# One decode layer on one core: 64 value rows multiplied on GpSimd, 8 key rows there, the head maximum by a VectorE transpose, one weight load cut by partitions

## The chip, the cores and the metric

The kernel runs on one core of a Trainium2 chip. The metric is the device time of one execution in microseconds; the kernel before has a median of 1319.2 us over 3 runs (1319.14 to 1319.23). Everything else comes from one execution that the hardware profiler recorded.

## The reference, cut to what matters

A decode step of one transformer layer with adaptive layer norm, batch 4, one token each, everything in float32:

```python
mod = (silu(c) @ w_mod).reshape(4, 6, 1, 512)            # sa, ca, ga, sb, cb, gb
h = layernorm(x) * (1 + ca) + sa
q = (h @ wq) -> (4, 32 heads, 1, 128)
scores = einsum("bhqd,bhkd->bhqk", q, k_cache) * 128 ** -0.5   # k_cache (4, 32, 4096, 128)
o = einsum("bhqk,bhkd->bhqd", softmax(scores), v_cache)        # v_cache (4, 32, 4096, 128)
x = x + ga * (o.reshape(4, 1, 4096) @ wo)
h = layernorm(x) * (1 + cb) + sb
x = x + gb * (silu(h @ w1) @ w2)                               # w1 (512, 1792), w2 (1792, 512)
```

The two caches hold 537 of the 567 MB that are read. Each cache element is used once: a key row of 128 floats gives one score, a value row is scaled by one weight and added up.

## The kernel before, in words

The caches are cut into 32 tiles each. Tile n stands for four heads (HP) of one batch row; t, b = n // 4, n % 4. A tile is 128 partitions x 128 rows x 128 floats, 64 KB in each partition and 8.4 MB in all. A partition holds 128 positions ("rows", index j) of one head; 32 partitions in a row belong to the same head. Three such buffers (the pool `kv`, class `Slot`) take turns, in the order k0, k1, v0, k2, v1, k3, ... So a key tile goes into the buffer of a value tile two steps older, and a value tile into that of the key tile just worked off. All loads are issued by SyncE (SP), in order, one whole tile at a time (`load_k`, `load_v`, `fetch`); an issue waits until the buffer is free.

The program's loop over n, whose order is the order on every engine, does in step n:

- Keys. Each row is multiplied by the query (`mult`) and summed over its 128 floats (`red`). GpSimd multiplies the first NA = 32 rows with a copy of the query in SBUF (`qw`), VectorE the other 96 with the query in PSUM (`qb`), and VectorE does all the sums into `sc[n]`. Steps 0 and 1 use NL = 56 rows in place of NA.
- Values of step n - 1. With `first(n)` = 14 groups of JJ = 4 rows, the first NV = 56 rows are scaled by their weights in place: rows 0 to 47 on GpSimd (one multiply), rows 48 to 55 on ScalarE (`vmult`). GpSimd then adds rows onto rows (28, 12, 8, 4 rows) until four are left, and TensorE sums these over the partitions in one matmul with `hs` (`vsum`). The other 72 rows go straight through TensorE: one matmul for each group of four (`pv`), with the weights spread into `pz` by GpSimd (in `softexp`). In the last two tiles, `first` is 0 and TensorE does all 128 rows.
- Softmax. `rowmax` gives a maximum for each partition; `bmax` transposes it on TensorE into PSUM, `negmax` takes the maximum of each head's 32 partitions and picks and negates it with the mask `hn` (three VectorE instructions); ScalarE does the exponentials (`softexp`).
- At three steps of four VectorE also drains or spreads a finished group of outputs (`gather`, `norm`, `spread`).

After the last key tile, SP loads `wo` in three pieces and the feed-forward weights `w12` in nine (w1 in the first two, then w2 in pieces of whole 512-column chunks, 256 KB each). TensorE matmuls named `busy` only fill time. The loop's last steps and the end of the program (projection, layer norm, the two feed-forward matmuls) run while these loads land; the last matmuls, of the second feed-forward matrix, take one chunk after the other.

Of the kernel before, what the change touches and what calls it, by code (L numbers as in the profile page):

```python
# [9 lines left out]
F32 = mybir.dt.float32  # L10
AF = mybir.ActivationFunctionType
ALU = mybir.AluOpType
AX = mybir.AxisListType
# [4 lines left out]
def kernel(  # L18
# [10 lines left out]
    nc = tc.nc  # L29
    P = 128  # L30
    B, H, S, Dh = kc.shape
    D = wo.shape[1] * P // (H * Dh)
    F = w12.shape[1] * P // (2 * D)
    G = 4
    W = P // G
    HP = 4
    QW = P // HP
# [6 lines left out]
    JJ = 4  # L44
# [4 lines left out]
    NK = D // P  # L49
    NI = F // P  # L50
    FG = F // G
    NA = 32
    NL = 56
    NV = 56
    NP = 48
    SCALE = 1.0 / math.sqrt(Dh)
    EPS = 1e-5
    N = B * NT
    SLOT = NJ * Dh

    const = ctx.enter_context(tc.tile_pool(name="const", bufs=1))
    kv = ctx.enter_context(tc.tile_pool(name="kv", bufs=3))
    work = ctx.enter_context(tc.tile_pool(name="work", bufs=2))
# [3 lines left out]
    def psum(shape, tag, bufs):  # L67
        return ps.tile(shape, F32, tag=tag, name=tag, bufs=bufs)
# [15 lines left out]
    def fetch(t, src, *cuts):  # L84
        for lo, hi in zip(cuts, cuts[1:]):
            nc.sync.dma_start(t[:, lo:hi], src[:, lo:hi])  # L86

    kt, vt = {}, {}

# [6 lines left out]
    def load_k(n, *cuts):  # L96
        load(kt, kc, "k", n, *cuts)

    def load_v(n):
        load(vt, vc, "v", n)  # L100
# [22 lines left out]
    ident = const.tile([P, P], F32, name="ident")  # L123
# [9 lines left out]
    avg = const.tile([P, G, W], F32, name="avg")  # L133
    for g in range(G):
        nc.vector.tensor_scalar(avg[:, g, :], sel, 1.0 / G, None, op0=ALU.mult)
    hm = const.tile([P, HP], F32, name="hm")
    nc.vector.tensor_reduce(hm, i4, axis=AX.X, op=ALU.add)
    hn = const.tile([P, HP], F32, name="hn")
    nc.vector.tensor_scalar(hn, hm, -1.0, None, op0=ALU.mult)
    jm = const.tile([P, JJ], F32, name="jm")  # L140
    nc.vector.tensor_reduce(jm, ident.rearrange("p (k j) -> p j k", j=JJ), axis=AX.X, op=ALU.add)
    xm = const.tile([P, B], F32, name="xm")
# [15 lines left out]
    hs = const.tile([P, W + E], F32, name="hs")  # L158
# [87 lines left out]
    for k in range(NK):  # L246
        for ch in range(H * Dh // CW):
            i, g = divmod(ch, G)
# [7 lines left out]
    for i in range(2):  # L256
        for u in range(HP):
            o = ZB - QW * u - G * B * i
# [9 lines left out]
    def make_qb(n):  # L268
        if n % B == 0:
            m = work.tile([P, B, Dh], F32, tag="o", name=f"qm{n}", bufs=1)  # L270
            for b in range(B):
                nc.scalar.activation(m[:, b, :], qn, AF.Copy, scale=sel[:, n + b : n + b + 1])  # L272
            p = psum([P, B, Dh], "q", 2)
            nc.tensor.matmul(p, blk.rearrange("p i x -> p (i x)"), m, start=True, stop=True)  # L274
            for b in range(B):
                qb[n + b] = p[:, b, :]
        qw[n] = work.tile([P, Dh], F32, tag="qw", name=f"qw{n}")
        nc.scalar.activation(qw[n], qb[n], AF.Copy)  # L278

    sc, nm, po, rs = {}, {}, {}, {}  # L280

    def mult(eng, src, n, lo, hi):
        eng.tensor_mul(  # L283
            kt[n][:, lo:hi, :], kt[n][:, lo:hi, :], src[n].unsqueeze(1).to_broadcast([P, hi - lo, Dh])
        )

    def red(n, lo, hi):
        nc.vector.tensor_reduce(sc[n][:, lo:hi], kt[n][:, lo:hi, :], axis=AX.X, op=ALU.add)  # L288

    def rowmax(n):  # L290
        nm[n] = work.tile([P, 1], F32, tag="rm", name=f"rm{n}")
        nc.vector.tensor_reduce(nm[n], sc[n], axis=AX.X, op=ALU.max)  # L292

    def bmax(n):
        p = psum([P, P + HP], "mx", 2)
        nc.tensor.transpose(p[:, :P], nm[n].to_broadcast([P, P]), ident)  # L296
        nm[n] = p

    def negmax(n):
        m = nm[n][:, P:]  # L300
        nc.vector.tensor_reduce(m, nm[n][:, :P].rearrange("p (i x) -> p i x", i=HP), axis=AX.X, op=ALU.max)  # L301
        nc.vector.tensor_mul(m, m, hn)
        nm[n] = work.tile([P, 1], F32, tag="nm", name=f"nm{n}")
        nc.vector.tensor_reduce(nm[n], m, axis=AX.X, op=ALU.add)  # L304

    def softexp(n):
        t, b = divmod(n, B)
        if b == 0:
            rs[t] = work.tile([P, B], F32, tag="rs", name=f"rs{t}")
        nc.scalar.activation(sc[n], sc[n], AF.Exp, bias=nm[n], accum_out=rs[t][:, b : b + 1])  # L310
        for h in range(2):
            f = min(max(first(n) - HG * h, 0), HG)
            m = HG - f
            if not m:
                continue
            nc.gpsimd.tensor_mul(  # L316
                pz[h][:, f * W : HG * W].rearrange("p (g x) -> p g x", g=m)[:, :, E:].rearrange("p g (i j) -> p g i j", i=HP),
                sc[n][:, JJ * (HG * h + f) : HG * JJ * (h + 1)].rearrange("p (g j) -> p g j", j=JJ)
                .unsqueeze(2).to_broadcast([P, m, HP, JJ]),
                hm.unsqueeze(1).unsqueeze(3).to_broadcast([P, m, HP, JJ]),  # L320
            )

    def first(n):
        return NV // JJ if n < N - 2 else 0

    def vmult(n):
        if first(n):
            v = vt[n]
            for j in range(NP, NV):
                nc.scalar.activation(v[:, j, :], v[:, j, :], AF.Copy, scale=sc[n][:, j : j + 1])  # L330
            nc.gpsimd.tensor_mul(  # L331
                v[:, :NP, :], v[:, :NP, :], sc[n][:, :NP].unsqueeze(2).to_broadcast([P, NP, Dh])
            )
            for m, lo in ((28, 28), (12, 16), (8, 8), (JJ, JJ)):
                nc.gpsimd.tensor_add(v[:, :m, :], v[:, :m, :], v[:, lo : lo + m, :])  # L335

    def vsum(n):
        t, b = divmod(n, B)
        q, a = divmod(b, 2)
        o = (1 - a) * E  # L340
        nc.tensor.matmul(  # L341
            po[t, q][0:W, :], hs[:, o : o + W], vt[n][:, :JJ, :].rearrange("p j d -> p (j d)"),
            start=False, stop=a == 1,
        )

    def pv(n):
        t, b = divmod(n, B)
        q, a = divmod(b, 2)
        if a == 0:
            po[t, q] = psum([P, JJ * Dh], "po", 2)  # L350
        f = first(n)
        for j in range(f, NG):
            g = j % G
            h, u = divmod(j, HG)
            o = u * W + (1 - a) * E
            nc.tensor.matmul(  # L356
                po[t, q][W * g : W * (g + 1), :],
                pz[h][:, o : o + W],
                vt[n][:, JJ * j : JJ * (j + 1), :].rearrange("p j d -> p (j d)"),
                start=(a == 0 and j < f + G), stop=(a == 1 and j >= NG - G and (g > 0 or not f)),  # L360
            )
# [25 lines left out]
    def sums(t):  # L387
        p = psum([P, B], "mx", 2)
        if t < TA:
            nc.tensor.matmul(p[W * t : W * (t + 1)], b8.rearrange("p i x -> p (i x)"), rs[t], start=True, stop=True)  # L390
        else:
            nc.tensor.matmul(p, blk.rearrange("p i x -> p (i x)"), rs[t], start=True, stop=True)
        rd[t] = p
# [53 lines left out]
    for n in range(N):  # L447
        t, b = divmod(n, B)
        if n + 1 < N:
            load_k(n + 1)  # L450
        else:
            load_v(n)
        if t and b == 1:
            sums(t - 1)
        sc[n] = work.tile([P, NJ], F32, tag="sc", name=f"sc{n}")
        w, m = (NJ // 2, NL // 2) if n == 0 else (NJ, NL) if n == 1 else (NJ, NA)
        for lo in range(0, NJ, w):
            mult(nc.gpsimd, qw, n, lo, lo + m)
            mult(nc.vector, qb, n, lo + m, lo + w)
            if n + 1 < N and not lo:  # L460
                make_qb(n + 1)
            if n:
                vmult(n - 1)
                pv(n - 1)
            red(n, lo + m, lo + w)
        for lo in range(0, NJ, w):
            red(n, lo, lo + m)
        if n + 1 < N:
            load_v(n)
        else:  # L470
            so = Slot("wo")
            wat, wot = so.take(RA, D), so.take(NT - TA, R, D)
            fetch(so.t, wo, 0, RA * D, SLOT - R * D, SLOT)
            s2 = Slot("w12")
            w1t = s2.take(NK, F)
            w2t = s2.take(NI, D)
            fetch(s2.t, w12, 0, 3 * F, *(NK * F + i * D for i in (0, 5, 8, 10, 11, 12, 13, 14)))
        rowmax(n)
        bmax(n)
        if n and first(n - 1):  # L480
            vsum(n - 1)
        negmax(n)
        softexp(n)
        if b == 3:
            gather(t, 0)
        if n == N - 1:
            sums(t)
            norm(t)
        if t and b == 1:
            gather(t - 1, 1)  # L490
            norm(t - 1)
        if t and b == 2:
            spread(t - 1)
# [25 lines left out]
    for g in range(G):  # L519
        o = g % 2 * P  # L520
# [71 lines left out]
```

## Time and profile before

| what | value |
|---|---|
| median of the runs shown | 1319.2 us |
| the profiled execution's own time | 1318.86 us |
| its span, first to last instruction | 1317.0 us |
| busy share of the span | DVE (VectorE) 79%, POOL (GpSimd) 82%, PE (TensorE) 27%, ACT (ScalarE) 10% |
| DMA queue of the loads | 99.6% of 16 DMA engines' span, 431 GB/s over the span |

The span is what the trace covers; 1.86 us of the execution lie outside it. "Idle before" in a group of instructions is the time in which the engine had nothing to run ahead of them, with what ended it. The time to landing of a load counts from its issue, so it holds the time that the load queued behind others.

### The profile page before, as it was taken

How to read it: one execution, taken by the hardware profiler on the slowest of the kernel's cores; microseconds unless marked ns; L12 is line 12 of the kernel's file. 1: busy time of each engine (PE TensorE's matmuls, PEld its weight loads, DVE VectorE, ACT ScalarE, POOL GpSimd, SP SyncE). 2: the span in 40 equal slices, each digit the busy share in tenths (PEclk: the TensorE clock that was granted, in tenths of full speed). 3: DMA queues.
4: the chain of work that ended last, by engine and by line, in shares of the span. 5: the costliest groups of instructions: out<-in, count | busy, mean ns of one | idle time of the engine just before them, and what ended most of it. 6: DMA issues, size and time to landing. Idle time of an engine off the chain costs nothing.

```text
span 1317.0 us, 5073 instructions
## 1 busy us (share of the span) xinstructions
PE 359.7 (27%) x1756; PEld 95.2 (7%) x1756; DVE 1045.5 (79%) x357; ACT 125.8 (10%) x408; POOL 1080.1 (82%) x257
## 2 busy tenths in 40 slices
PE   3301322221222232122322122132312213221258
PEld 1100000000000000000000000000000000000013
DVE  2597788988878998788898888789887878978762
ACT  1100110010001101011100100000100010000001
POOL 0459888888988888998888899888889888888910
PEclk9856666656666665666665566666556666655669
DMA  9999999999999999999999999999999999999998
GB/s 415 440 420 444 428 435 434 426 442 434 430 440 428 438 435 428 438 434 432 430 442 432 430 439 432 434 434 430 438 432 432 438 432 434 436 432 438 428 426 349
DMA packets 11433, 567.63 MB, mean 431 GB/s; under 512 B 1280, under 2 KB 1296, under 8 KB 2192
## 3 DMA queue, kind: packets, MB, share of 16 engines
q1 hardware_dynamic: 11408, 567.31, 99.6%
q8 instruction: 14, 0.23, 0.1%
q14 instruction: 11, 0.09, 0.0%
HBM read 567.30 MB, written 0.01 MB: 431 GB/s over the span
## 4 chain that ended last, share of the span: by engine, by line
DMA 50%; DVE 27%; POOL 19%; PE 2%; issue 1%; ACT 0%; SPq 0%; DVEq 0%; POOLq 0%
DMA k<-in_A_k_cache_dram 23%; DMA v<-in_A_v_cache_dram 21%; DVE sc L288 16%; DVE k L283 11%; POOL v L335 11%; POOL v L331 8%; DMA w<-in_B_w_dram 3%; DMA wq<-in_A_wq_dram 3%; PE po L341 1%; PE q L249 1%; PE mx L259 0%; ACT qm L272 0%; PE q L274 0%; SPq L86 0%; PE od L378 0%
## 5 line engine op out<-in xcount | busy, mean ns | idle before, releaser
L288 DVE TENSOR_REDUCE sc<-k 128x96 f32<-128x12288 f32 (+3 forms) x66 | 553.1, 8422 | 4.1
L283 DVE TENSOR_TENSOR k<-k,q 128x12288 f32<-128x12288 f32 (+2 forms) x33 | 408.3, 12372 | 183.1 <-DMA k<-in_A_k_cache_dram 168.1
L335 POOL TENSOR_TENSOR v<-v 128x3584 f32<-128x3584 f32 (+1 forms) x120 | 443.8, 3698 | 9.4
L331 POOL TENSOR_TENSOR v<-v,sc 128x6144 f32<-128x6144 f32 x30 | 313.8, 10460 | 103.4 <-DMA v<-in_A_v_cache_dram 103.4
L283 POOL TENSOR_TENSOR k<-k,qw 128x4096 f32<-128x4096 f32 (+2 forms) x33 | 296.4, 8982 | 31.4 <-ACT qw L278 31.4
L356 PE MATMUL po<-v,pz 128*32 128x512 f32 x1208 | 216.3, 839 | 335.6 <-DMA v<-in_A_v_cache_dram 335.6
L341 PE MATMUL po<-v,hs 128*32 128x512 f32 x60 | 57.4, 1061 | 413.8 <-POOL v L335 413.8
L330 ACT ACTIVATE v<-v,sc 128x128 f32<-128x128 f32 x240 | 73.6, 389 | 199.3 <-DMA v<-in_A_v_cache_dram 199.3
L356 PEld LDWEIGHTS po<-v,pz 128*32 128x32 f32 x1208 | 56.1, 148 | 500.8 <-issue 482.3
L296 PE MATMUL mx<-ident,rm 128*128 128x128 f32 x32 | 12.7, 396 | 175.7 <-DVE rm L292 175.7
L278 ACT ACTIVATE qw<-q 128x128 f32<-128x128 f32 x32 | 8.9, 278 | 525.6 <-DVE k L283 424.0
L316 POOL TENSOR_TENSOR pz<-sc,hm 128x32 f32<-128x32 f32 (+1 forms) x64 | 26.7, 438 | 30.4 <-ACT sc L310 30.4
L310 ACT ACTIVATE sc<-sc,nm 128x128 f32<-128x128 f32 x32 | 12.9, 402 | 367.9 <-DVE nm L304 367.9
L341 PEld LDWEIGHTS po<-v,hs 128*32 128x32 f32 x60 | 5.4, 140 | 421.5 <-POOL v L335 421.5
L301 DVE TENSOR_REDUCE mx<-mx 128x4 f32<-128x128 f32 x32 | 9.6, 300 | 17.8 <-PE mx L296 17.8
L367 DVE TENSOR_TENSOR o<-po,jm 128x512 f32<-128x512 f32 x16 | 10.9, 681 | 13.6 <-PE po L356 13.6
L296 PEld LDWEIGHTS mx<-ident,rm 128*128 128x128 f32 x32 | 5.2, 163 | 203.9 <-issue 162.1
L373 DVE TENSOR_REDUCE s<-o 128x128 f32<-128x512 f32 x16 | 16.5, 1034 | 0.6
L274 PE MATMUL q<-qm,blk 128*128 128x512 f32 x16 | 15.6, 1073 | 1.7 <-ACT qm L272 1.7
L200 PE MATMUL q<-wm 128*32 128x512 f32 x48 | 8.9, 668 | 18.9 <-DVE wm L184 18.9
L190 POOL COPY wm<-wm 128x16 f32<-128x16 f32 x1 | 0.2, 212 | 16.0 <-DMA wm<-in_head_dram 16.0
L499 PE MATMUL q<-mod,ident 128*128 128x512 f32 (+2 forms) x24 | 10.7, 554 | 0.0
(114 smaller groups left out, 164.9 us busy)
## 6 DMA issues: line engine op xcount, KB each, us to landing
k<-in_A_k_cache_dram SPq DMA_DIRECT2D x2, 4096.0 KB, 51.1
wm<-in_head_dram SPq DMA_DIRECT2D x1, 6160.0 KB, 17.7
wo<-in_A_wo_dram SPq DMA_DIRECT2D x1, 4096.0 KB, 18.1
wo<-in_A_wo_dram SPq DMA_DIRECT2D x1, 3072.0 KB, 25.0
w<-in_B_w_dram SPq DMA_DIRECT2D x1, 2688.0 KB, 33.1
w<-in_B_w_dram SPq DMA_DIRECT2D x1, 1280.0 KB, 37.3
wo<-in_A_wo_dram SPq DMA_DIRECT2D x1, 1024.0 KB, 27.0
w<-in_B_w_dram SPq DMA_DIRECT2D x4, 256.0 KB, 17.6
```

The costliest lines, as they stand in the source:

```text
L249: nc.tensor.matmul(pq[i][W * g : W * (g + 1), :], hT[:, k, :], wqt[:, k, ch * CW : (ch + 1) * CW], start=k == 0, stop=k == NK - 1,)
L274: nc.tensor.matmul(p, blk.rearrange("p i x -> p (i x)"), m, start=True, stop=True)
L283: eng.tensor_mul(kt[n][:, lo:hi, :], kt[n][:, lo:hi, :], src[n].unsqueeze(1).to_broadcast([P, hi - lo, Dh]))
L288: nc.vector.tensor_reduce(sc[n][:, lo:hi], kt[n][:, lo:hi, :], axis=AX.X, op=ALU.add)
L296: nc.tensor.transpose(p[:, :P], nm[n].to_broadcast([P, P]), ident)
L316: nc.gpsimd.tensor_mul(pz[h][:, f * W : HG * W].rearrange("p (g x) -> p g x", g=m)[:, :, E:].rearrange("p g (i j) -> p g i j", i=HP), sc[n ...
L330: nc.scalar.activation(v[:, j, :], v[:, j, :], AF.Copy, scale=sc[n][:, j : j + 1])
L331: nc.gpsimd.tensor_mul(v[:, :NP, :], v[:, :NP, :], sc[n][:, :NP].unsqueeze(2).to_broadcast([P, NP, Dh]))
L335: nc.gpsimd.tensor_add(v[:, :m, :], v[:, :m, :], v[:, lo : lo + m, :])
L341: nc.tensor.matmul(po[t, q][0:W, :], hs[:, o : o + W], vt[n][:, :JJ, :].rearrange("p j d -> p (j d)"), start=False, stop=a == 1,)
L356: nc.tensor.matmul(po[t, q][W * g : W * (g + 1), :], pz[h][:, o : o + W], vt[n][:, JJ * j : JJ * (j + 1), :].rearrange("p j d -> p (j d)") ...
L373: nc.vector.tensor_reduce(s, o.rearrange("p j d -> p d j"), axis=AX.X, op=ALU.add)
```

## The change

Four edits. `hm` is also given 64 bytes in place of 16, and `hn` is gone; the tile buffers start at the same addresses as before.

- Keys: NA = 8, so VectorE multiplies 120 rows of a tile and GpSimd 8 (steps 0 and 1 stay at 56).
- Values: GpSimd multiplies NV = 64 rows in tiles 0 to 29 and adds 32, 16, 8 and 4 rows; the last add writes to a tile of its own, `vs`, which `vsum` reads. ScalarE scales none. TensorE does 64 rows through `pv`. Tile 30 gets NU = 32 rows of this kind; tile 31 none.
- Maximum: `bmax` is gone. `negmax` transposes 32 x 32 blocks on VectorE, takes one maximum and negates it.
- Chunks 5 to 7 of w2 are loaded by partitions, 112, 12 and 4 of them; the chunks behind go as 3, 2 and 1 in place of 2, 1, 1, 1, 1.

```diff
-    NA = 32
+    NA = 8
-    NV = 56
-    NP = 48
+    NV = 64
+    NU = 32
...
+    def by_rows(t, src, lo, hi, *counts):
+        at = 0
+        for m in counts:
+            nc.sync.dma_start(t[at : at + m, lo:hi], src[at : at + m, lo:hi])
+            at += m
...
-    def bmax(n):
-        p = psum([P, P + HP], "mx", 2)
-        nc.tensor.transpose(p[:, :P], nm[n].to_broadcast([P, P]), ident)
-        nm[n] = p
-
     def negmax(n):
-        m = nm[n][:, P:]
-        nc.vector.tensor_reduce(m, nm[n][:, :P].rearrange("p (i x) -> p i x", i=HP), axis=AX.X, op=ALU.max)
-        nc.vector.tensor_mul(m, m, hn)
-        nm[n] = work.tile([P, 1], F32, tag="nm", name=f"nm{n}")
-        nc.vector.tensor_reduce(nm[n], m, axis=AX.X, op=ALU.add)
+        m = work.tile([P, QW], F32, tag="hx", name=f"hx{n}")
+        nc.vector.transpose(m, nm[n].to_broadcast([P, QW]))
+        nm[n] = work.tile([P, 2], F32, tag="nm", name=f"nm{n}")
+        nc.vector.tensor_reduce(nm[n][:, 0:1], m, axis=AX.X, op=ALU.max)
+        nc.vector.tensor_scalar(nm[n][:, 1:2], nm[n][:, 0:1], -1.0, None, op0=ALU.mult)
...
     def first(n):
-        return NV // JJ if n < N - 2 else 0
+        return (NV if n < N - 2 else NU if n < N - 1 else 0) // JJ
...
     def vmult(n):
-        if first(n):
-            v = vt[n]
-            for j in range(NP, NV):
-                nc.scalar.activation(v[:, j, :], v[:, j, :], AF.Copy, scale=sc[n][:, j : j + 1])
-            nc.gpsimd.tensor_mul(
-                v[:, :NP, :], v[:, :NP, :], sc[n][:, :NP].unsqueeze(2).to_broadcast([P, NP, Dh])
-            )
-            for m, lo in ((28, 28), (12, 16), (8, 8), (JJ, JJ)):
-                nc.gpsimd.tensor_add(v[:, :m, :], v[:, :m, :], v[:, lo : lo + m, :])
+        v, m = vt[n], JJ * first(n)
+        nc.gpsimd.tensor_mul(v[:, :m, :], v[:, :m, :], sc[n][:, :m].unsqueeze(2).to_broadcast([P, m, Dh]))
+        vs[n] = work.tile([P, JJ, Dh], F32, tag="vs", name=f"vs{n}", bufs=1)
+        while m > JJ:
+            m //= 2
+            nc.gpsimd.tensor_add(vs[n] if m == JJ else v[:, :m, :], v[:, :m, :], v[:, m : 2 * m, :])
...
-            fetch(s2.t, w12, 0, 3 * F, *(NK * F + i * D for i in (0, 5, 8, 10, 11, 12, 13, 14)))
+            wc = [NK * F + i * D for i in range(NI + 1)]
+            fetch(s2.t, w12, 0, 3 * F, wc[0], wc[5])
+            by_rows(s2.t, w12, wc[5], wc[8], 112, 12, 4)
+            fetch(s2.t, w12, wc[8], wc[11], wc[13], wc[14])
         rowmax(n)
-        bmax(n)
-        if n and first(n - 1):
+        if n:
             vsum(n - 1)
         negmax(n)
```

Three places show how this moves instructions. The first is GpSimd in the middle of the program, from the weights' spread of one step to that of the next. Before (pz, sc, k, qw and v are the tiles named above; the number tells one step's tile from another's):

```order
L316 TENSOR_TENSOR pz_113<-sc_404,hm 128x2x16
L316 TENSOR_TENSOR pz_114<-sc_404,hm 128x16x16
L283 TENSOR_TENSOR k_402<-k_402,qw_414 128x4096
L331 TENSOR_TENSOR v_450<-v_450,sc_404 128x6144
L335 TENSOR_TENSOR v_450<-v_450 128x3584
L335 TENSOR_TENSOR v_450<-v_450 128x1536
L335 TENSOR_TENSOR v_450<-v_450 128x1024
L335 TENSOR_TENSOR v_450<-v_450 128x512
```

And the same step of the changed kernel:

```order
L315 TENSOR_TENSOR pz_112<-sc_378,hm 128x16x16
L287 TENSOR_TENSOR k_376<-k_376,qw_388 128x1024
L327 TENSOR_TENSOR v_415<-v_415,sc_378 128x8192
L331 TENSOR_TENSOR v_415<-v_415 128x4096
L331 TENSOR_TENSOR v_415<-v_415 128x2048
L331 TENSOR_TENSOR v_415<-v_415 128x1024
L331 TENSOR_TENSOR vs_444<-v_415 128x512
```

The key multiply shrinks to a quarter, the value multiply and the adds grow, the last add leaves the value tile, and the small spread into the first `pz` is gone.

The second is VectorE in the same part, one step's keys and softmax maximum (rm is the maximum of each partition, nm the negated one, mx the PSUM tile). Before:

```order
L283 TENSOR_TENSOR k_473<-k_473,q 128x12288
L288 TENSOR_REDUCE sc_532<-k_473 128x96
L288 TENSOR_REDUCE sc_532<-k_473 128x32
L292 TENSOR_REDUCE rm_573<-sc_532 128x1
L301 TENSOR_REDUCE mx<-mx 128x4
L302 TENSOR_TENSOR mx<-mx,hn 128x4
L304 TENSOR_REDUCE nm_580<-mx 128x1
```

The changed kernel (hx is the transposed tile in SBUF):

```order
L287 TENSOR_TENSOR k_436<-k_436,q 128x15360
L292 TENSOR_REDUCE sc_484<-k_436 128x120
L292 TENSOR_REDUCE sc_484<-k_436 128x8
L296 TENSOR_REDUCE rm_516<-sc_484 128x1
L300 STREAM_TRANSPOSE hx_519<-rm_516 128x32
L302 TENSOR_REDUCE nm_521<-hx_519 128x1
L303 TENSOR_SCALAR nm_521<-nm_521 128x1
```

VectorE now has all but 8 rows to multiply, and its maximum no longer goes through TensorE and PSUM; source and result of the new L300, L302 and L303 lie in SBUF.

The third is SP's queue at the end, with what each issue waits for (PE, DVE, Activation, Pool: that engine has done with the buffer; DMAHW: an earlier load has landed). Before:

```order
L86 DMA v_2153<-in_A_v_cache_dram 128x16384 [waits DMAHW7_49,PE_49,Activation_49]
L86 DMA wo<-in_A_wo_dram 128x8192 [waits DMAHW0_49,DVE_49]
L86 DMA wo<-in_A_wo_dram 128x6144
L86 DMA wo<-in_A_wo_dram 128x2048
L86 DMA w_2197<-in_B_w_dram 128x5376 [waits DMAHW1_49,PE_49]
L86 DMA w_2197<-in_B_w_dram 128x1792
L86 DMA w_2197<-in_B_w_dram 128x2560
L86 DMA w_2197<-in_B_w_dram 128x1536
L86 DMA w_2197<-in_B_w_dram 128x1024 [waits DMAHW2_49]
```

The changed kernel:

```order
L86 DMA v_1820<-in_A_v_cache_dram 128x16384 [waits DMAHW7_49,PE_49,Pool_49]
L86 DMA wo<-in_A_wo_dram 128x8192 [waits DMAHW1_49,PE_49,Pool_49]
L86 DMA wo<-in_A_wo_dram 128x6144
L86 DMA wo<-in_A_wo_dram 128x2048
L86 DMA w_1861<-in_B_w_dram 128x5376 [waits DMAHW0_49,DVE_49]
L86 DMA w_1861<-in_B_w_dram 128x1792
L86 DMA w_1861<-in_B_w_dram 128x2560
L91 DMA w_1861<-in_B_w_dram 112x1536
L91 DMA w_1861<-in_B_w_dram 12x1536 [waits DMAHW2_49]
L91 DMA w_1861<-in_B_w_dram 4x1536 [waits DMAHW3_49]
```

`wo` now goes into the buffer of value tile 30, which GpSimd has to finish, and `w12` into that of key tile 31; before it was the other way round. A load into a value tile's buffer (all the key loads, and v31 here) waits for GpSimd's adds and the matmuls of `pv`, where before it also waited for `vsum`.

More of the change, by code (lines that the diff above doesn't have):

```diff
@@ L135 @@
         nc.vector.tensor_scalar(avg[:, g, :], sel, 1.0 / G, None, op0=ALU.mult)
-    hm = const.tile([P, HP], F32, name="hm")
+    hm = const.tile([P, 4 * HP], F32, name="hm")[:, :HP]
     nc.vector.tensor_reduce(hm, i4, axis=AX.X, op=ALU.add)
-    hn = const.tile([P, HP], F32, name="hn")
-    nc.vector.tensor_scalar(hn, hm, -1.0, None, op0=ALU.mult)
     jm = const.tile([P, JJ], F32, name="jm")
@@ L278, in make_qb @@
         nc.scalar.activation(qw[n], qb[n], AF.Copy)
-    sc, nm, po, rs = {}, {}, {}, {}
+    sc, nm, po, rs, vs = {}, {}, {}, {}, {}
     def mult(eng, src, n, lo, hi):
@@ L309, in softexp @@
             rs[t] = work.tile([P, B], F32, tag="rs", name=f"rs{t}")
-        nc.scalar.activation(sc[n], sc[n], AF.Exp, bias=nm[n], accum_out=rs[t][:, b : b + 1])
+        nc.scalar.activation(sc[n], sc[n], AF.Exp, bias=nm[n][:, 1:2], accum_out=rs[t][:, b : b + 1])
         for h in range(2):
@@ L341, in vsum @@
         nc.tensor.matmul(
-            po[t, q][0:W, :], hs[:, o : o + W], vt[n][:, :JJ, :].rearrange("p j d -> p (j d)"),
+            po[t, q][0:W, :], hs[:, o : o + W], vs[n].rearrange("p j d -> p (j d)"),
             start=False, stop=a == 1,
```

## The prediction

> **What bounds the kernel now.** I read the page first: the bandwidth by slices, the queues, and the times from issue to landing.
>
> ```profile
> span 1317.0 us, 5073 instructions
> ...
> GB/s 415 440 420 444 428 435 434 426 442 434 430 440 428 438 435 428 438 434 432 430 442 432 430 439 432 434 434 430 438 432 432 438 432 434 436 432 438 428 426 349
> ...
> q1 hardware_dynamic: 11408, 567.31, 99.6%
> q8 instruction: 14, 0.23, 0.1%
> ...
> v<-in_A_v_cache_dram SPq DMA_DIRECT2D x32, 27.4
> k<-in_A_k_cache_dram SPq DMA_DIRECT2D x31, 30.3
> out_dram<-end SPq DMA_DIRECT2D x1, 8.0 KB, 1.8
> ```
>
> The loads' queue fills 99.6% of the DMA engines' span, and no slice but the last falls under 415 GB/s. The kernel is bound by its loads; VectorE and GpSimd at some 80% follow. So the question is whether the queue still always holds the next tile. The timeline of one step tells by how much it does.
>
> ```profile
> 599.13 10.46 POOL L331 TENSOR_TENSOR v<-v,sc 128x6144 f32<-128x6144 f32 x1 [3.45 <-DMA v<-in_A_v_cache_dram]
> ...
> 610.22 0.33 SPq L86 DMA_DIRECT2D v<-in_A_v_cache_dram  x1
> 610.23 0.29 DVE L292 TENSOR_REDUCE rm<-sc 128x1 f32<-128x128 f32 x1
> ...
> 611.68 0.16 DVE L304 TENSOR_REDUCE nm<-mx 128x1 f32<-128x4 f32 x1
> ...
> 612.60 1.01 DVE L420 TENSOR_REDUCE oa<-v 32x64 f32<-32x512 f32 x1
> ...
> 618.38 12.95 DVE L283 TENSOR_TENSOR k<-k,q 128x12288 f32<-128x12288 f32 x1 [4.77 <-DMA k<-in_A_k_cache_dram]
> ...
> 624.75 1.91 PE L341 MATMUL po<-v,hs 128*32 128x512 f32 x2 [13.65 <-POOL v L335]
> ...
> 626.74 0.33 SPq L86 DMA_DIRECT2D k<-in_A_k_cache_dram  x1
> ...
> 637.73 10.46 POOL L331 TENSOR_TENSOR v<-v,sc 128x6144 f32<-128x6144 f32 x1 [3.46 <-DMA v<-in_A_v_cache_dram]
> ```
>
> GpSimd starts a value tile as it lands: 599.13, 637.73. A step, two tiles, takes 38.6 us, one tile 19.3. The key load issued at 626.74 follows the value tile that lands at 637.6, so it is issued some 11 us ahead of need, and the median says the same: 30.3 - 19.3 = 11.0. A value load is ahead by 27.4 - 19.3 = 8.1 us. These two leads are what the change can spend for nothing. Prices come from the groups by shape.
>
> ```profile
> L283 DVE TENSOR_TENSOR k<-k,q 128x12288 f32<-128x12288 f32 x30 | 388.6, 12954 | 168.1 <-DMA k<-in_A_k_cache_dram 168.1
> L288 DVE TENSOR_REDUCE sc<-k 128x96 f32<-128x12288 f32 x30 | 388.6, 12953 | 4.0
> L331 POOL TENSOR_TENSOR v<-v,sc 128x6144 f32<-128x6144 f32 x30 | 313.8, 10460 | 103.4 <-DMA v<-in_A_v_cache_dram 103.4
> L283 POOL TENSOR_TENSOR k<-k,qw 128x4096 f32<-128x4096 f32 x30 | 265.5, 8852 | 0.0
> L335 POOL TENSOR_TENSOR v<-v 128x3584 f32<-128x3584 f32 x30 | 232.0, 7733 | 2.4
> ...
> L288 DVE TENSOR_REDUCE sc<-k 128x32 f32<-128x4096 f32 x30 | 132.3, 4409 | 0.0
> L335 POOL TENSOR_TENSOR v<-v 128x1536 f32<-128x1536 f32 x30 | 103.0, 3434 | 2.4
> ...
> L335 POOL TENSOR_TENSOR v<-v 128x1024 f32<-128x1024 f32 x30 | 70.7, 2356 | 2.4
> ...
> L335 POOL TENSOR_TENSOR v<-v 128x512 f32<-128x512 f32 x30 | 38.1, 1269 | 2.4
> ...
> L283 POOL TENSOR_TENSOR k<-k,qw 128x7168 f32<-128x7168 f32 x1 | 15.3, 15331 | 0.0
> L283 DVE TENSOR_TENSOR k<-k,q 128x4608 f32<-128x4608 f32 x2 | 9.9, 4950 | 14.7 <-ACT qw L278 14.7
> ```
>
> **The change part by part.** *Values on GpSimd.* Adds: 3584 to 512 elements cost 7.73 to 1.27 us, 2.10 ns an element, so 4096, 2048, 1024 and 512 cost 8.81, 4.51, 2.36 and 1.27, together 16.95. The multiply of 8192 has no row. At its own rate it takes 10.46 x 8192 / 6144 = 13.95; at the key multiply's step, (15.33 - 8.85) / 3072 = 2.11 ns, the 2048 more take 4.3 and the sum is 14.8. With the fixed part of the key rows (8.85 - 4096 x 2.11 ns = 0.2) it is 13.9; I take that, since it is the same operation with the same operands, and keep 13.9 to 14.8. With four gaps of 0.07 a value tile is done 13.9 + 16.95 + 0.3 = 31.1 us after landing, before 25.6 (599.13 to 624.75). The key load behind it no longer waits for the two matmuls at 624.75 (1.9 us). So it is issued 31.1 us after the landing where it was 27.6: the lead goes from 11.0 to 7.5, or 6.6 at the dearer multiply. GpSimd's key multiply falls to 8.85 - 3072 x 2.11 ns = 2.4, and with the remaining spread of about 0.6 its step is 34 to 35 us of 38.6: hidden by the 4 us that remain.
>
> *Keys on VectorE.* An element costs (12.954 - 4.950) / 7680 = 1.042 ns. 15360 elements take 16.16, for the product and for the sum, and the last 8 rows about 1.2: 33.5 in place of 12.95 + 12.95 + 4.41 = 30.3. The value load waits for exactly this, so its lead falls by 3.2, from 8.1 to 4.9 us. VectorE's wait for keys (168.1 us over 30, 5.6 a step) shrinks by the same 3.2, to 2.4 or more. The cover is gone only if something adds 2 to 3 us on VectorE in every step.
>
> *Maximum.* The old chain runs from 610.23 to 611.84, 1.6 us. The new one keeps the first 0.29 and adds a transpose of 32 columns, a reduction and a negation of one element. The old small reductions are 0.16 each and the transpose of 128 columns below is 0.31, so 0.15 to 0.31 for the transpose: 0.9 to 1.1 in all, a gain of some 0.6 on VectorE, under its wait. The negation is the open price; it is the first rival.
>
> *ScalarE and TensorE* lose 8 scalings a step, the transpose and two matmuls of 18. Both mostly wait for landings; nothing on the path.
>
> *The end.*
>
> ```profile
> 1257.00 9.15 PE L356 MATMUL po<-v,pz 128*32 128x512 f32 x64 [11.11 <-DMA v<-in_A_v_cache_dram]
> ...
> 1268.01 1.28 SPq L86 DMA_DIRECT2D wo<-in_A_wo_dram  x3
> ...
> 1276.53 9.62 PE L356 MATMUL po<-v,pz 128*32 128x512 f32 x64 [4.54 <-DMA v<-in_A_v_cache_dram]
> ...
> 1313.27 0.43 PE L543 MATMUL po<-w,end 128*32 128x128 f32 x8 [0.20 <-DMA w<-in_B_w_dram]
> ```
>
> Tile 30 lands at 1256.9. GpSimd multiplies 32 of its rows (4096 elements, 7.0 to 8.9 us by the same two rates) and adds 16, 8 and 4 (8.1), done by 1272.4 to 1274.2; `wo` now waits for that in place of 1268.0. The last value tile is still landing until 1276.5, so `wo` is 2.3 to 4.1 us ahead: free. The wait holds up the eleven weight loads behind it on SP, all needed later. Key tile 31 is summed 3.2 later, at about 1271.3, its weights are spread by about 1274.5, under the landing at 1276.5. The last matmuls wait for the last landing (1313.27), and the last piece is the same 256 KB.
>
> *The load by partitions.* The same 768 KB, and nine loads of `w12` as before. If the 16 DMA engines get uneven parts, by one row of 6144 bytes, an engine's end moves by 6144 B / (431 / 16 GB/s) = 0.23 us, to either side. I take 0. [...]
>
> *Instruction loads.* 14 packets on q8 pass between the data on some engine. Steps vary. Two value tiles 27 steps apart on the chain of waits,
>
> ```profile
> 135.13 10.47 POOL v L331
> ...
> 1179.77 10.47 POOL v L331
> ```
>
> give 1044.6 us, 38.69 a step, 0.09 over the one above, some 2.8 us over 31 steps. TensorE's instructions shrink by about a tenth; if these packets are the cause, that gives 0.2 to 0.3, and if they fall elsewhere, 0 to 2.8.
>
> **Sum.** 0 in the steps, 0 at the end, -0.2: 1318.7 against the profiled execution's 1318.86, which is 0.3 below the median. Against the median it is 1319.0.
>
> **The rivals.**
>
> *VectorE blocked by GpSimd, slower.* In steady state the kernel before gives VectorE no copy or scaling from SBUF to SBUF. The first microseconds have some:
>
> ```profile
> 1.39 1.01 POOL L157 MEMSET pz<- 128x528 f32 x2
> ...
> 1.92 0.50 DVE L132 COPY selb<-sel 128x4 f32<-128x4 f32 x1
> ...
> 3.02 0.16 DVE L143 COPY xm<-sel 128x4 f32<-128x4 f32 x1
> ```
>
> Four elements take 0.16 us alone and 0.50 beside a GpSimd memset: the copy ends at 2.42, just after the memset does (2.40). If the negation L303 is held like that, it meets GpSimd 15.2 us after the value's landing (the sums end at 610.2 - 599.1 + 3.2 = 14.3), in the add of 4096 that runs from 14.0 to 22.9: 7.7 us lost in every step. VectorE then takes up the next key tile 23.0 us after that landing where the tile is there at 19.3, and 24.8 after a gather or spread (the spread behind 611.84 ends at 613.61). Its sums end 33.6 later, at 58.4; with a microsecond from issue to the first byte (the output's whole way takes 1.8) and 19.3 of transfer the next value but one lands at 78.7, against two steps of 77.2 to 77.4. That is 0.7 us for each of some 23 such steps, 16 us, and 3 at the end: about 1338. It decides from a delay of about 4 us (the lead of 4.9 less that microsecond); a plain step, 3.7 late, loses nothing. Against it:
>
> ```profile
> 880.54 7.74 POOL L335 TENSOR_TENSOR v<-v 128x3584 f32<-128x3584 f32 x1
> ...
> 884.51 0.16 DVE L410 RECIPROCAL rd<-rd 128x1 f32<-128x1 f32 x1
> ...
> 1228.90 15.02 POOL L335 TENSOR_TENSOR v<-v 128x3584 f32<-128x3584 f32 x4
> ...
> 1231.22 0.31 DVE L427 STREAM_TRANSPOSE ot<-on 128x128 f32<-128x128 f32 x1
> ```
>
> One element from SBUF to SBUF, and a transpose, run unhindered in the middle of a GpSimd add. The one-element reciprocal is the nearest row to the negation, so I take 0.16 and keep 7.7. [...]
>
> *Faster by the instruction packets.* All 2.8 us and the 0.23 go: 1316.2. For it, the irregular steps; against it, nine tenths of the instructions stay.
>
> *A wait at the end, slower.* If `wo` comes after 1276.5 or the last weights' spread does, the excess adds up directly: GpSimd would have to be 2.3 us later than the dearest price, and 3 more give 1322.0.
>
> *The change does not do what it says*: cutting by partitions moves no load. That is within the 0.23.
>
> **Chances.** No change (within 0.2%, 2.6 us, about what a measurement tells from none) 0.82; VectorE blocked with a loss 0.12, the late end 0.02: slower 0.14; faster 0.04. The range 1316.8 to 1321.6 takes in most of the 2.8 below and, above, an instruction packet more on the slowest engine, 0.23, and a late end; it leaves out the blocked case and little else.
>
> **What the profile after would show.** Median times to landing near 26.8 for keys and 24.2 for values, with the queue still at 99.6%; the value multiply at 13.9 and L303 at 0.16. VectorE waiting for keys some 70 to 90 us in all instead of 168. If L303 takes microseconds, or the wait for keys is gone, the blocked case has come; if a slice in the middle falls under 415 GB/s, a lead was too short.

## The result, and the profile after

The changed kernel takes 1323.3 us (median of 9 runs, 1321.65 to 1327.15) against 1319.2 for the kernel before (9 runs, 1319.07 to 1319.65): a ratio of 1.0034, 95% interval 1.0025 to 1.0043. The forecast was 1319.0 within 1316.8 to 1321.6, with 0.82 on no change. It was wrong: the kernel became slower, and the median lies above the range.

The profiled execution took 1321.65 us, the least of the nine; its span is 1319.9, 2.9 more than before, so the trace shows 2.9 of the 4.1 us that the medians lie apart. The page of the changed kernel, with the times to landing from its view of the DMA queues:

```profile
span 1319.9 us, 4424 instructions
...
GB/s 414 437 421 443 435 426 441 435 427 441 430 433 439 429 433 439 431 433 431 429 441 431 431 440 427 437 437 427 439 433 429 441 431 429 441 431 431 441 419 316
...
q1 hardware_dynamic: 11136, 567.31, 99.5%
...
v<-in_A_v_cache_dram SPq DMA_DIRECT2D x32, 24.2
k<-in_A_k_cache_dram SPq DMA_DIRECT2D x31, 26.7
```

No slice between the first and the last two falls below 421, and the queue's share is 99.5%. The times to landing are those foretold (24.2 and 26.8). Only the last slice has lost much: 316 where it was 349. The groups by shape of the changed kernel show the steps:

```profile
L287 DVE TENSOR_TENSOR k<-k,q 128x15360 f32<-128x15360 f32 x30 | 484.6, 16155 | 95.0 <-DMA k<-in_A_k_cache_dram 95.0
...
L303 DVE TENSOR_SCALAR nm<-nm 128x1 f32<-128x1 f32 x32 | 4.9, 154 | 1.1
...
L327 POOL TENSOR_TENSOR v<-v,sc 128x8192 f32<-128x8192 f32 x30 | 416.5, 13884 | 135.4 <-DMA v<-in_A_v_cache_dram 135.4
L331 POOL TENSOR_TENSOR v<-v 128x4096 f32<-128x4096 f32 x30 | 265.1, 8836 | 2.4
```

The third column, the idle time before a group, is what a reader looks at first: in the steps both engines still wait for nothing but landings (95.0 and 135.4 us). The negation takes 154 ns in the mean of 32. One step in the timeline of the changed kernel shows that the negation isn't held while GpSimd is adding:

```profile
613.50 15.89 POOL L331 TENSOR_TENSOR v<-v 128x4096 f32<-128x4096 f32 x3
613.78 0.33 SPq L86 DMA_DIRECT2D v<-in_A_v_cache_dram  x1
614.57 0.15 DVE L303 TENSOR_SCALAR nm<-nm 128x1 f32<-128x1 f32 x1
...
630.77 0.33 SPq L86 DMA_DIRECT2D k<-in_A_k_cache_dram  x1
638.15 13.88 POOL L327 TENSOR_TENSOR v<-v,sc 128x8192 f32<-128x8192 f32 x1 [4.52 <-DMA v<-in_A_v_cache_dram]
```

The negation at 614.57 lies 1 us into a GpSimd add and costs 0.15. The key load is issued at 630.77, 7.4 us before the value tile ahead of it is taken up (638.15), as foretold (7.5).

So the loss has to lie behind the steps. The timeline's rows of the last value tile and of the last weight piece, after:

```profile
1276.47 9.87 PE L352 MATMUL po<-v,pz 128*32 128x512 f32 x64 [1.15 <-DMA v<-in_A_v_cache_dram]
...
1316.14 0.43 PE L541 MATMUL po<-w,end 128*32 128x128 f32 x8 [0.30 <-DMA w<-in_B_w_dram]
```

TensorE takes up the last value tile at 1276.47 (before 1276.53): the first 1276 us of this execution, with the three edits of the loop in them, came out even. The last weight piece, the same 256 KB, lands 2.9 us later (1316.14 against 1313.27). The chain of waits puts it down to one transfer; first before, then after (start, length, what):

```profile
1302.47 10.75 DMA w<-in_B_w_dram
```

```profile
1302.39 13.71 DMA w<-in_B_w_dram
```

The last load is issued 0.08 earlier and takes 2.96 longer. The bandwidth in 40 slices of the stretch from 1295 to 1320 (0.625 us each) shows where it was lost, before and after:

```profile
GB/s 405 447 413 447 482 356 401 451 356 393 388 411 426 477 408 396 400 459 400 423 393 410 403 367 279 282 226 174 23 0 0 0 0 13 0 0 0 0 0 0
```

```profile
GB/s 529 378 447 378 482 447 447 287 482 344 344 478 433 436 405 492 364 419 256 243 246 226 226 246 246 206 288 400 413 344 187 85 29 0 0 0 0 13 0 0
```

After the change nine slices from the nineteenth on, 1306.25 to 1311.9, run at 206 to 288, in the mean 243, and then the rate is back at 400. At 434, the rate of the steps (the row from 600 to 1100 below), their 1.37 MB would have taken 3.1 us instead of 5.6: 2.5 of the 2.9 us. Were the engines out of work? The windows from 1306 to 1312, before and after (the last three columns are TensorE's clock, the DMA engines' busy share, and GB/s; a transfer counts in the window in which it starts, so a share can come out a little above 1):

```profile
1306.00:1312.00 6.00, 5.56 (x108) 3.28 (x104) 1.56 (x2) 0.54 (x1) 0.00 (x0) 1.00 0.90 358
```

```profile
600.00:1100.00 500.00, 112.50 (x468) 26.48 (x460) 458.39 (x120) 16.98 (x61) 438.46 (x91) 0.56 1.00 434
...
1306.00:1312.00 6.00, 4.70 (x60) 1.97 (x52) 1.57 (x2) 0.54 (x1) 0.00 (x0) 1.00 1.02 257
```

They were not: a share of 1.02 with 257 GB/s. The 16 engines are busy the whole time and move little, so each transfer takes longer (0.42 us in the median for a row of 6144 bytes from 1306.25 to 1311.9, 0.23 before). In the kernel before the share falls to 0.90 here since its queue runs out of bytes. What lies in the stretch are the three loads of 112, 12 and 4 partitions, 786 KB together, and loads beside them in the queue.

### The profile page after: what moved, and what is told of

Read it like the earlier page. It is cut to its first block, busy times and chain, and to the rows that moved or that the text cites. A ratio compares the mean times of both kernels' runs of the same rounds, so it can differ in the third digit from the quotient of the medians.

```text
span 1319.9 us, 4424 instructions
## 1 busy us (share of the span) xinstructions
PE 325.2 (25%) x1590; PEld 83.1 (6%) x1590; DVE 1138.7 (86%) x356; ACT 52.3 (4%) x168; POOL 1062.9 (81%) x231
## 3 DMA queue, kind: packets, MB, share of 16 engines
q1 hardware_dynamic: 11136, 567.31, 99.5%
## 4 chain that ended last, share of the span: by engine, by line
DMA 45%; DVE 30%; POOL 23%; PE 1%; issue 1%; ACT 0%; DVEq 0%; POOLq 0%; SPq 0%
DMA k<-in_A_k_cache_dram 20%; DMA v<-in_A_v_cache_dram 19%; DVE sc L292 16%; DVE k L287 14%; POOL v L331 12%; POOL v L327 11%; DMA w<-in_B_w_dram 3%; DMA wq<-in_A_wq_dram 3%; POOL vs L331 1%; PE q L253 1%; PE mx L263 0%; ACT qm L276 0%; PE q L278 0%; DVE s L369 0%; DVE o L363 0%
## 5 line engine op out<-in xcount | busy, mean ns | idle before, releaser
L287 DVE TENSOR_TENSOR k<-k,q 128x15360 f32<-128x15360 f32 (+2 forms) x33 | 504.3, 15282 | 109.3 <-DMA k<-in_A_k_cache_dram 95.0
L292 DVE TENSOR_REDUCE sc<-k 128x120 f32<-128x15360 f32 (+3 forms) x66 | 553.1, 8422 | 3.6 <-DVE k L287 0.5
L327 POOL TENSOR_TENSOR v<-v,sc 128x8192 f32<-128x8192 f32 (+1 forms) x31 | 423.5, 13663 | 139.6 <-DMA v<-in_A_v_cache_dram 139.6
L331 POOL TENSOR_TENSOR v<-v 128x2048 f32<-128x2048 f32 (+2 forms) x92 | 478.5, 5201 | 7.2
L337 PE MATMUL po<-vs,hs 128*32 128x512 f32 x62 | 59.3, 1061 | 770.5 <-POOL vs L331 770.5
L352 PE MATMUL po<-v,pz 128*32 128x512 f32 x1072 | 192.0, 883 | 192.5 <-DMA v<-in_A_v_cache_dram 192.5
L287 POOL TENSOR_TENSOR k<-k,qw 128x1024 f32<-128x1024 f32 (+2 forms) x33 | 101.6, 3079 | 31.4 <-ACT qw L282 31.4
L331 POOL TENSOR_TENSOR vs<-v 128x512 f32<-128x512 f32 x31 | 39.3, 1269 | 2.4
L315 POOL TENSOR_TENSOR pz<-sc,hm 128x256 f32<-128x256 f32 (+1 forms) x34 | 20.5, 607 | 13.9 <-ACT sc L309 13.9
L276 ACT ACTIVATE qm<-qn,sel 128x128 f32<-128x128 f32 x32 | 10.2, 389 | 4.9 <-DVE oa L416 4.8
```

Of the source, the lines that this page charges most:

```text
L287: eng.tensor_mul(kt[n][:, lo:hi, :], kt[n][:, lo:hi, :], src[n].unsqueeze(1).to_broadcast([P, hi - lo, Dh]))
L315: nc.gpsimd.tensor_mul(pz[h][:, f * W : HG * W].rearrange("p (g x) -> p g x", g=m)[:, :, E:].rearrange("p g (i j) -> p g i j", i=HP), sc[n ...
L327: nc.gpsimd.tensor_mul(v[:, :m, :], v[:, :m, :], sc[n][:, :m].unsqueeze(2).to_broadcast([P, m, Dh]))
L331: nc.gpsimd.tensor_add(vs[n] if m == JJ else v[:, :m, :], v[:, :m, :], v[:, m : 2 * m, :])
L337: nc.tensor.matmul(po[t, q][0:W, :], hs[:, o : o + W], vs[n].rearrange("p j d -> p (j d)"), start=False, stop=a == 1,)
L352: nc.tensor.matmul(po[t, q][W * g : W * (g + 1), :], pz[h][:, o : o + W], vt[n][:, JJ * j : JJ * (j + 1), :].rearrange("p j d -> p (j d)") ...
```

## The experiments

The theory: the cut by partitions makes the loads slow, and nothing else in the change costs time. The rivals: the shares of the engines are uneven (the 12 and 4 rows); the leads were made too short; more loads in the queue cost by themselves.

**e1_columns**: the whole change, with the cut undone.

```diff
-            by_rows(s2.t, w12, wc[5], wc[8], 112, 12, 4)
+            fetch(s2.t, w12, wc[5], wc[6], wc[7], wc[8])
```

> The changed kernel with one edit undone: chunks 5 to 7 of w2 come as three loads of 128 partitions, one chunk each, so that there are still nine loads of w12. Theory A (the cut by partitions runs at a lower rate and loses the time at the end): about 1319.0 to 1319.3 us, and the spread between runs shrinks to that of the kernel before (under 1 us). Theory B (shorter leads of the tile loads cost it): stays at 1322 to 1324. Theory C (any smaller loads at the end cost a fixed time each): three small loads stay, so 1321 or more.

1319.92 us (1319.17 to 1321.94, 11 runs), ratio 1.0007 (0.9998 to 1.0015). The loss is gone up to 0.7 us, which the interval doesn't tell from none. The window of the same stretch:

```profile
1306.00:1312.00 6.00, 5.56 (x88) 2.75 (x80) 1.56 (x2) 0.54 (x1) 0.00 (x0) 1.00 1.02 411
```

The same share and 411 GB/s in place of 257. That the runs lie 2.8 us apart, against 1.0 for the kernel before beside them, was not expected.

**e2_cut_alone**: the kernel before, with nothing but the cut (and `by_rows` for it) and the chunks behind it as 3, 2 and 1.

```diff
-            fetch(s2.t, w12, 0, 3 * F, *(NK * F + i * D for i in (0, 5, 8, 10, 11, 12, 13, 14)))
+            wc = [NK * F + i * D for i in range(NI + 1)]
+            fetch(s2.t, w12, 0, 3 * F, wc[0], wc[5])
+            by_rows(s2.t, w12, wc[5], wc[8], 112, 12, 4)
+            fetch(s2.t, w12, wc[8], wc[11], wc[13], wc[14])
```

> The kernel before with the cut by partitions alone (112, 12 and 4, and the chunks behind as 3, 2, 1). A: 1322 to 1326 us, with runs several us apart. B: 1319.2, since keys, values and maximum are those of before.

1323.58 us (1323.33 to 1323.62, 5 runs), ratio 1.0033 (1.0020 to 1.0045). The cut alone costs what the whole change costs.

```profile
1306.00:1312.00 6.00, 4.19 (x45) 1.65 (x41) 1.57 (x2) 0.54 (x1) 0.00 (x0) 1.00 1.01 240
```

240 GB/s at a share of 1.01. The expected spread of the runs did not come: they lie 0.3 us apart. So the cut gives the median of the change, and the spread of the change's runs (5.5 us) is from something else.

**e3_112_16**: 112 and 16 partitions, both multiples of the 16 DMA engines.

```diff
-            by_rows(s2.t, w12, wc[5], wc[8], 112, 12, 4)
+            by_rows(s2.t, w12, wc[5], wc[8], 112, 16)
```

> The changed kernel with the counts 112 and 16 in place of 112, 12 and 4, so that the two parts divide evenly among 16 DMA engines (7 and 1 rows each). A in the form that uneven shares of the engines cost the time: 1319.3. A in the form that any cut that shifts the partitions of each engine costs it: 1321.5 to 1325.

1323.05 us (1321.40 to 1324.77, 9 runs), ratio 1.0029 (1.0019 to 1.0039).

```profile
1306.00:1312.00 6.00, 5.40 (x48) 1.89 (x52) 1.67 (x3) 1.13 (x3) 0.00 (x0) 1.00 1.02 273
```

The counts now divide evenly among 16, and the loss stays: counts that don't aren't its cause. Which rows an engine takes, no trace shows. That leaves loads of fewer than 128 partitions; how much of the loss is the load of 112 and how much the load of 16, this run doesn't tell.

**e4_tiles_64_64**, **e6_tiles_112_16** and **e7_tiles_columns** make the cut larger: the cut at the end undone, and four key tiles (8 to 11, 8.4 MB each) loaded in two parts, by partitions or, as the control, by columns (in the lines below, the comment stands for the edits of e6 and e7).

```diff
-        fetch(dst[n], src, *(cuts or (0, NJ)))
+        if dst is kt and 8 <= n < 12:
+            by_rows(dst[n], src, 0, NJ, 64, 64)     # e6: 112, 16; e7: fetch(dst[n], src, 0, NJ // 2, NJ)
+        else:
+            fetch(dst[n], src, *(cuts or (0, NJ)))
```

> To measure a rate: e1_columns, with key tiles 8 to 11 (8.4 MB each) loaded as partitions 0 to 63 and 64 to 127. Engines get even shares, 4 rows of 64 KB in each half. If a cut by partitions only matters where shares are uneven or rows are small: 1319.2 and 434 GB/s in those stretches. [...]

1417.19 us (1410.95 to 1423.43, 2 runs), ratio 1.0743 (1.0699 to 1.0786): 97.3 us above e1, where four tiles at half of 434 GB/s would cost some 77 more (an estimate, 19.3 us for each). Windows of this kernel, in the first cut tile and long after the last:

```profile
330.00:350.00 20.00, 6.01 (x32) 1.48 (x32) 15.42 (x8) 1.19 (x4) 18.58 (x2) 0.59 0.98 204
...
600.00:1000.00 400.00, 85.75 (x364) 19.37 (x364) 368.44 (x93) 12.62 (x45) 346.27 (x75) 0.56 1.00 434
```

204 GB/s in the cut tile, a little under half of the 434 that whole tiles have, with the engines busy in both.

> Key tiles 8 to 11 loaded as 112 and 16 partitions. If 112 partitions run at about half rate, as the packets at the end of the changed kernel did (some 0.43 us in place of 0.23 for 6 KB): the 7.3 MB take about 31 us and the 16 rows 2.4 to 4.8, so 14 to 17 us more a tile, 1375 to 1390. If the halves in e4 were slow only because they cover half of the partitions, 112 of 128 cost little: under 1335.

1422.84 us (1416.28 to 1429.39, 2 runs), ratio 1.0787 (1.0741 to 1.0832).

```profile
330.00:350.00 20.00, 6.11 (x32) 1.49 (x32) 15.48 (x8) 1.19 (x4) 19.15 (x2) 0.59 1.03 259
```

The total is above both expectations, and the window shows part of why: in the load of 112 partitions 259 GB/s, better than the 204 of 64 in the same stretch, but far from 434. The load of 16 that follows is worse. The trace also holds every single transfer of the DMA engines, one row of one partition each, with its start and duration. A row of 64 KB of a whole tile takes 2.42 us; from 326 to 350 of this run the median is 4.49; and the 17 rows that start from 355 to 363, when the load of 16 is due, take 7.4 to 9.3 us. The trace doesn't name a row's load; that these are in the main the load of 16 is inferred from their place.

> Control for e4: the same key tiles in two loads of 128 partitions, each half of the columns (32 KB of a row). All theories of partitions: as e1_columns, 1319 to 1322. If two loads for one tile, or smaller rows, cost the time: near 1417.

1320.32 us (1319.84 to 1321.90, 8 runs), ratio 1.0013 (1.0003 to 1.0023), 0.4 above e1_columns.

```profile
328.00:333.00 5.00, 4.32 (x24) 1.23 (x28) 5.00 (x1) 0.00 (x0) 4.32 (x1) 0.50 1.05 452
```

Two loads of 128 partitions each, of the same bytes as in e4: 452 in this short window, which is the full rate; in the median their rows of 32 KB take 1.21 us, half of the 2.42 for 64 KB. So it isn't the number of loads, nor their size.

**e5_tiles_32_64_32** asks whether what counts is how many partitions a load has, or which. It is e4 with `by_rows(dst[n], src, 0, NJ, 32, 64, 32)`: the middle load has 64 partitions too, from 32 to 95.

> As e4_tiles_64_64, but key tiles 8 to 11 are loaded as partitions 0 to 31, 32 to 95 and 96 to 127. The middle load has as many rows for each engine as a half in e4, from rows shifted by 32. [...] If any load of fewer than 128 partitions runs at half rate, or the order of the rows in memory sets it: all three at half, about 1400 to 1417 as in e4.

1420.78 us (1410.90 to 1430.67, 2 runs), ratio 1.0771 (1.0703 to 1.0840). The total is above the 1400 to 1417 expected if all three loads run at half the rate. In the first cut tile the window of 338 to 346 shows 354 GB/s where e4 has 207, so something ran faster. Why four cut tiles in a row cost this much all the same wasn't followed up; the totals of e4 and e6 also lie above what half the rate gives.

**e9_one_64_64** and **e10_one_32_64_32** therefore cut one tile alone (`if dst is kt and n == 8`), the cut at the end undone.

> As e4_tiles_64_64, but only key tile 8 is cut, so that no tile behind it is cut as well and the buffers can recover. If halves run at half rate: some 20 to 25 us more, 1340 to 1345 us.

> As e5_tiles_32_64_32, but only key tile 8 is cut. If the rate depends on which partitions are written at a time, the middle load is at the full rate and only the outer 4.2 MB at half: about half the loss of e9_one_64_64, 1329 to 1335 us. If any load of fewer than 128 partitions is slow, or the order of rows in memory is the cause: the same loss as e9_one_64_64.

e9: 1342.34 us (1341.41 to 1346.72, 3 runs), ratio 1.0185 (1.0169 to 1.0201). e10: 1337.23 (1335.62 to 1340.76, 3 runs), ratio 1.0142 (1.0127 to 1.0158), above the 1329 to 1335 expected if the partitions decide and below e9. The windows answer better than the totals. e9, the first half (the second window runs on some 2 us into the other) and the second half:

```profile
326.00:336.00 10.00, 3.65 (x20) 1.12 (x24) 9.90 (x2) 0.28 (x1) 3.65 (x1) 0.66 1.05 223
338.00:348.00 10.00, 0.00 (x0) 0.00 (x0) 8.47 (x8) 1.19 (x4) 9.92 (x2) 0.73 0.98 203
348.00:358.00 10.00, 0.00 (x0) 0.00 (x0) 0.00 (x0) 0.00 (x0) 9.92 (x2) 0.50 1.02 210
```

e10, mainly the partitions 0 to 31, 32 to 95 and 96 to 127 in turn:

```profile
326.00:336.00 10.00, 5.66 (x32) 1.42 (x32) 10.00 (x1) 0.00 (x0) 6.28 (x1) 0.61 1.03 216
338.00:348.00 10.00, 0.00 (x0) 0.00 (x0) 6.87 (x8) 1.19 (x4) 9.92 (x2) 0.63 1.14 406
348.00:358.00 10.00, 0.00 (x0) 0.00 (x0) 0.00 (x0) 0.00 (x0) 9.84 (x3) 0.50 0.85 177
```

Two loads of 64 partitions, the same number of rows and bytes: 203 to 223 GB/s from 0 to 63 and from 64 to 127, 406 from 32 to 95. Windows of 10 us are coarse for transfers of 2 to 5; the single rows of 64 KB are sharper. In e9 they take 5.12 us (median from 329 to 363, in both halves). In e10 they take 5.13 in the first load (327 to 333), 2.42 in the middle one (338 to 345), exactly that of whole tiles, and 5.12 in the last (349 to 356). The rows 32 to 63, from the same place in memory into the same partitions, are slow together with 0 to 31 and fast together with 64 to 95. What decides is which rows are moved together. That it is the partitions written, and not the places in memory read, isn't separated: no run moved the same rows into other partitions.

**e8_keys_alone**, **e11_keys_20** and **e12_max_alone** are the kernel before with one of the other edits: `NA = 8`, `NA = 20` (halfway between 8 and 32), and the maximum by the transpose of VectorE. The edit of the values has no run of its own; it stands in e1, together with the other two.

> The kernel before with 8 key rows on GpSimd in place of 32 and nothing else. Only the lead of the value loads shrinks, from 8.1 to 4.9 us. If short leads are what spreads the times of e1_columns (1319.17 to 1321.94) against those of the kernel before (under 1 us): median 1319.3 to 1320.0 with a spread of 1.5 us or more. If they cost nothing: 1319.2 and a spread under 1 us.

> The kernel before with 20 key rows on GpSimd in place of 32 and nothing else: the lead of the value loads is about 6.5 us, between those of the kernel before (8.1) and of e8_keys_alone (4.9). If the lead sets how far the times spread: median 1319.1 to 1319.6 and a spread of 1 to 2 us, between 0.8 and 2.7. If it does not: as e8_keys_alone or as before, without order.

> The kernel before with the maximum by a VectorE transpose and nothing else. Neither a lead nor a load changes: 1319.0 to 1319.3 with a spread under 1 us. If the negation from SBUF to SBUF were held by GpSimd: 7.7 us on VectorE in each step, still within its wait for keys of 5.6 and the lead of 8.1, up to 1321.

| kernel | median, us | runs | ratio (95%) | value load, issue to landing |
|---|---|---|---|---|
| e8_keys_alone | 1320.02 | 1318.89 to 1321.58 (11) | 1.0008 (0.9999 to 1.0017) | 24.3 us |
| e11_keys_20 | 1319.18 | 1318.57 to 1319.52 (11) | 1.0000 (0.9991 to 1.0009) | 25.8 us |
| e12_max_alone | 1319.17 | 1318.62 to 1319.49 (11) | 1.0000 (0.9991 to 1.0009) | 27.4 us |

The maximum costs and brings nothing. A lead of 25.8 - 19.3 = 6.5 us costs nothing either. At 5.0 the runs of e8 lie 2.7 us apart (0.8 for the kernel before beside it) and the median is 1.0 higher, which its interval doesn't tell from no change. The runs of e1 and of the changed kernel, with the same lead, are as wide or wider.

The single rows of the trace show something that goes with the short lead. Over all rows of 64 KB, the time above the usual 2.418 us, shared over 16 engines, adds up to 0.6 to 0.7 us in the profiled executions of the kernel before, e2, e11 and e12, and to 0.95, 1.7, 2.2 and 2.0 in those of the changed kernel, e1, e3 and e8, the four that have the short lead and whole tiles. In the changed kernel 49 of the 8192 rows take over 50 ns more than usual, 10 of them starting within 3 us (from 577.6); in the kernel before 26 do, never more than 2 within 3 us. Whether the short lead causes them, and how, is not shown.

## Why the prediction was wrong, and where it was right

*The load by partitions* is the step that failed: "I take 0", with 0.23 us to either side. It measured 2.5 to 2.9 us in the profiled execution, some 3.4 by medians (1323.3 - 1319.92, after against e1), and 4.3 by itself (e2). The step weighed how many bytes each of the 16 DMA engines gets, took their rate from the whole tiles (431 / 16 GB/s each), and concluded that the same bytes take the same time. The shares were not the trouble, since with counts that divide evenly among 16 (e3) the loss is the same; the rate was. In the single transfers of the trace a row of 6144 bytes takes 0.42 us in the stretch (median from 1306.25 to 1311.9), where 0.23 is usual. The nearest rows were no fair bound: every load of the kernel before writes all 128 partitions, so the trace had nothing on a load that doesn't. A price that no row shows was given the width of a small calculation in place of the width of what wasn't known. The share of the chances went wrong with it: of 0.14 on slower, none stood for this.

What the runs show of the cause: from 1306 to 1312 the DMA engines are busy throughout (a share of 1.01 to 1.02 in the changed kernel, e2 and e3) and move 240 to 273 GB/s, where e1 moves 411. The rate depends on which partitions a load covers, with the reserve said under e10, not on the count of loads (e7), of rows (e9 against e10) or on whether 16 divides the counts (e3). Loads of one half of the partitions, 0 to 63 or 64 to 127, ran at 203 to 223 GB/s (e9), whole tiles at 434; the load of 32 to 95, with rows of both halves, ran at 406, and its single rows took as long as in whole tiles (2.42 us, e10). Rows of both halves are not enough for the full rate: the load of 112 in e6 has all of the first half and 48 of the second, and ran at 259. Why the halves are slow, and why the 112 are, no run shows.

The slow stretch of the profiled execution (1.37 MB) holds more than the 786 KB of the cut loads, so their neighbours in the queue were slow as well. The single rows show it: in e2, 49 of the 128 rows of 10,240 bytes, which only the whole load ahead of the cut ones has, take 0.62 to 0.86 us where 0.385 is usual. Added up over the rows of w2, the time above the usual, shared over 16 engines, is 2.5 us in the changed kernel, 4.0 in e2, 2.7 in e3, and nothing in the kernel before and in e1 (under 0.05). This is most of the loss of each (2.9 of span in the changed kernel, 4.6 in e2), and the neighbours are where e2 lost more: 1.6 of its 4.0 lies in rows that are not of the cut loads' size, 0.2 of 2.5 in the changed kernel. The same holds for e9: 128 rows at 5.12 in place of 2.42 make 21.6 us over 16 engines, and it is 22.4 above e1. Why the neighbours were slowed more in e2 is open.

*Values on GpSimd* came out as worked out: 13.884 (taken 13.9), adds from 8.836 (8.81) down, a key lead of 26.7 - 19.3 = 7.4 (7.5).

*Keys on VectorE*: 16.155 (16.16). The landing of values at 24.2 is to the tenth. The wait for keys is 95.0 in all, above the 70 to 90 foretold and far from gone; it was reckoned too pessimistically by 5 us over 30 steps. But "These two leads are what the change can spend for nothing" is only half shown: a lead of 6.5 us costs nothing (e11), and with 5 the runs spread and the rows of whole tiles take 2.0 us more than usual in all (e8). The median cost, 0.7 to 1.0 us, isn't told from none, and no run took the lead of values below 4.9.

*The maximum*: the negation takes 153 to 155 ns all 32 times, so VectorE isn't blocked, which was the main rival (1338, 0.12). The gain of 0.6 on VectorE went under its wait, and e12 shows no change.

*The end*: `wo` is issued at 1272.4, the lower of the two times worked out, and hides as said. *Instruction packets*: 12 on q8 in place of 14, and the last value tile is taken up 0.06 earlier; the 0.2 can't be told from this. The signs that the text named for a failure did not come: L303 stayed short, the wait for keys stayed, and no slice in the middle fell under 415 GB/s. The loss shows in the last slice, of which the text said nothing.

## What to carry to other kernels

Cut a load by columns, not by partitions: four key tiles cut by columns cost 0.4 us over e1 (e7), by partitions 97 to 103 (e4, e5, e6). A DMA busy share near 1 at half of the usual GB/s was the sign of it (0.98 at 204 in e4, 1.00 at 434 for whole tiles); a queue that ran out of bytes showed in the share instead (0.90 from 1306 to 1312 in the kernel before). A change with three edits in the loop and one behind it is read by the landing of the last tile of the loop: if that hasn't moved, nothing in the loop did it in that execution. And where every row of the trace has one shape, a load of another shape has no price: its bound is then not the small calculation that one can do, but the worst that the resource could do.

## What the runs showed of the hardware

- A row of 64 KB takes a DMA engine 2.42 us in a load of 128 partitions and in one of the partitions 32 to 95, and 5.12 to 5.13 us in loads of 0 to 63, 64 to 127, 0 to 31 and 96 to 127 (e9, e10). In GB/s that is 434 for whole tiles and 203 to 223 for the halves.
- The load of 112 partitions of a tile of 8.4 MB ran at 259 GB/s (e6, 330 to 350): sixteen partitions fewer than all cost 40% of the rate of 434.
- A slow load slows a whole load beside it: 0.62 to 0.86 us for 49 of the 128 rows of 10,240 bytes in e2, where 0.385 is usual.
- A one-element scaling from SBUF to SBUF on VectorE takes 153 to 155 ns, with 31 of the 32 inside a GpSimd instruction (one of them the add at 613.50), where the 128 x 4 copy beside a memset, in the prediction, took 0.50 us.
- A GpSimd multiply by a weight that is broadcast over 128 elements takes 13,884 ns for 8192 elements, 1.69 ns each, against 2.16 for the add of 4096 (8,836 ns).
